# Raw attention scores of three chunks: two heads on the two row halves of the array, packed queries, narrower first tiles

## The chip, the cores and the metric

One core of a Trainium2 chip runs the whole program. The metric is the device time of one execution in microseconds (us), taken as the median of several runs. The engines are TensorE (PE, with its weight loads listed as PEld), VectorE (DVE), ScalarE (ACT), GpSimd (POOL) and SyncE (SP); SP and POOL also issue DMAs from their queues, in program order.

## What is computed

Sliding-window attention with a few sink columns, followed by a two-layer block over the 4 x 768 tokens. Cut to what matters:

```python
# q, k, v: (4, 8, 768, 64) float32; n_sink = 4, window = 128
scores = (q @ k.T) / 8                      # per head
keep = (pos_k < n_sink) | ((0 <= pos_q - pos_k) & (pos_q - pos_k < window))
a = exp(where(keep, scores, -1e9) - rowmax); a /= sum(a) + 1e-9
x = (a @ v) laid out as (3072, 512)         # 8 heads x 64 side by side
h = x @ w_in                                # (512, 2048)
out = (h - tanh(h)) @ w_out                 # (2048, 512)
```

## The kernel before, in words

**Work units.** The tokens are cut into 12 chunks of 256 (`NCHUNK`), each with 4 units (one per pair of heads), so unit `u` is chunk `u // 4`, head pair `u % 4`. The chunk list starts with the first chunks of three batches (chunks 0 to 2); those twelve units are the `raw(u)` ones (`RAW = 12`): their scores are one float32 matmul per head. All later units are first split into a rounded part and a rest (`split`, L464) and take two fp32r matmuls per head (L514).

**Scores of a unit** (`scores`, L497). A unit has two tiles of 128 queries, t = 0 and t = 1. The keys lie packed with the four sink columns repeated in front of every block (`TS = 132`, `WIN = 260`, `KW = 392` columns). A key tile holds the two heads of a pair in partitions 0 to 63 and 64 to 127. The query tile is `[128, 2, 256]`: for head h the other 64 partitions are zeros, so that a matmul over all 128 rows gives one head's scores:

```python
nc.tensor.matmul(ps[h][:, :WIN], lhsT=qt[u][:, h, t * P : (t + 1) * P],
                 rhs=kt[u][:, t * TS : t * TS + WIN], start=True, stop=True)
```

Head 0 goes to one PSUM bank and head 1 to another (banks s0 and s1 for t = 0, o0 and o1 for t = 1). `kind = min(2 * c + t, 2)`; for the raw units c = 0, so t = 0 is kind 0 and t = 1 is kind 1. `merge` on DVE (L529, L531) masks and takes the row minimum: with kind 0 it reads only columns 128 to 259 of the bank, with kind 1 it first copies columns 0 to 127 over others under a mask. Then ACT takes the exponent (L539), DVE the sums (L559, L560), ACT or POOL scales (L565, L569), POOL copies the sink columns (L574 to L576), PE transposes (L599), ACT, DVE and POOL mask and copy (L606, L613), and per two or four units `attend` (L632) does the sink and value matmuls: L656 over all 512 columns, L662 with 64 weight columns per head, so that the two heads of a pair lie on the two column halves of the array.

**Loads of a raw unit.** Units 0 and 1 are loaded ahead of the branch (L70 to L73) into `early`; `_load_pair` (L97) zeroes half of the query tile on POOL (L103) and sends one DMA per head (L104). For units 2 to 11, `load_qk` (L319) adds a POOL memset of the whole query tile (`zeros`, L348), a key DMA (L337) and `queries` (two DMAs, L344 by way of L104), both on SP. Units 4 to 11 lie in places lent by weight tiles that come later (`lent`, L309). For later units both loads go from POOL's queue (L337, L346).

**The two-layer block.** A step `n` is (chunk, weight group g of 8). Its first half is 24 fp32r matmuls of 256 columns (L793), then ACT and DVE form h - tanh(h) and split it (L812 to L821), and its second half is 12 matmuls of 512 columns (L863) or, from chunk `SA = 5` on, 21 matmuls of 256 columns (L897). The order starts with chunks 0, 1, 2 at g = 0, then at g = 1, then chunks 2 and 1 at each later g, then chunk 0 at g = 2 to 7, then chunks 3 to 11. The weights arrive as 64-bit words (L392) and are decoded on DVE in three passes (L156 to L160), rounded on ACT (L717) and their rest taken on DVE (L721). From chunk 3 on the first-layer weights are streamed from a scratch in DRAM by SP (L778) through seven ring blocks, four per step. From chunk 5 on the weights of the edge products are derived by SP and POOL DMAs, ACT and DVE (L982 to L1021). Results of the chunks 5 to 10 are stored from POOL's queue (`put`, L951, `ST = 1`).

**What sets the order.** `Work` (L169) is a planner at build time. Every piece of work has an engine, an estimated duration, a due time, and what it reads and writes. `order` (L194) plays the program: whenever an engine is free it takes, of the pieces that are ready, the one with the earliest due time; the resulting order is written out by hand on each engine. The due times come from the constants at L261 to L276 (`FIRST`, `EARLY`, `PACE`, `LEAD`, `LEAD3`, `UNIT`, `SECOND`, ...) by `due_step`, `due_unit` and `due_group`. So a constant does not delay work by itself; it decides which of several ready pieces goes first, and in what order a queue holds them.

Of the kernel before, what the change touches and what calls it, by code (L numbers as in the profile page):

```python
# [40 lines left out]
def kernel(  # L41
# [20 lines left out]
    for m in range(2):  # L62
        first = pts[:, m].rearrange("p h a b -> p (h a b)")
        early.append((first[:, :KW], first[:, KW : KW + 2 * CH].rearrange("p (h s) -> p h s", h=2)))
    et = mybir.EngineType
    with tc.manual_schedule(engines={et.PE, et.SP, et.DVE, et.Activation, et.Pool}):
# [3 lines left out]
        for m in range(2):  # L70
            k, q = early[m]
            nc.sync.dma_start(k, kp[0, m, :, :KW])
            _load_pair(nc, q, qd[0, 2 * m : 2 * m + 2, :, :CH], True)  # L73
            if m == 0:
                make_identity(nc, ident)
                nc.gpsimd.iota(scr[:, 0, :].bitcast(I32), pattern=[[-1, P]], base=0, channel_multiplier=1)
                nc.gpsimd.iota(scr[:, 1, :].bitcast(I32), pattern=[[1, P]], base=0, channel_multiplier=0)
# [19 lines left out]
def _load_pair(nc, q, src, zeros):  # L97


    for h in range(2):  # L100
        r, z = slice(64 * h, 64 * h + 64), slice(64 * (1 - h), 64 * (1 - h) + 64)
        if zeros:
            nc.gpsimd.memset(q[z, h, :], 0.0)  # L103
        nc.sync.dma_start(q[r, h, :], src[h, r])  # L104
# [128 lines left out]
def _banded(tc, qd, kp, vp, vs, masks, w_in, w_out, ident, pts, early, out):  # L233
    nc = tc.nc
    et = mybir.EngineType
    with ExitStack() as ctx:
# [25 lines left out]
        SLK, PAD, LATE, LAND, QP, KP, BP, LEAD3 = 0.0, 1.05, 65222.0, 4372.0, 0, 0, 1, 89032.0  # L262
        SA, NSLOT, RING, GP, LQ, ST = 5, 7, 7, 0, 1, 1
# [9 lines left out]
        FIRST, EARLY, PACE, LEAD = 45000.0, 4600.0, 8242.0, 72963.0  # L273
        UNIT, SECOND, WLEAD, WNEXT = 2000.0, 3000.0, 6000.0, 2500.0
        HALF2, LAST = 8269.0, 4401.0
        SPILL, STREAM, DEAR, DLATE = 54590.0, 4000.0, 39769.0, 31275.0  # L276
# [42 lines left out]
        def load_qk(u):  # L319
# [12 lines left out]
            def keys():  # L332
                if u in lent or u == 3:
                    kt[u] = lend()[:, 2 * CH : 2 * CH + KW]
                else:
                    kt[u] = kpool.tile([P, KW], F32, tag="kraw", name=f"kraw{u}")
                (nc.gpsimd if LQ and not raw(u) else nc.sync).dma_start(kt[u], kp[b, p, :, 2 * c * TS : 2 * c * TS + KW])  # L337

            def queries():
                if not raw(u):  # L340
                    qt[u] = qpool.tile([P, 2, CH], F32, tag="qraw", name=f"qraw{u}")
                src = qd[b, 2 * p : 2 * p + 2, :, c * CH : (c + 1) * CH]
                if raw(u):
                    _load_pair(nc, qt[u], src, False)  # L344
                else:
                    (nc.gpsimd if LQ else nc.sync).dma_start(qt[u], src.rearrange("h d s -> d h s"))  # L346

            def zeros():  # L348
                if u in lent or u == 3:
                    qt[u] = lend()[:, : 2 * CH].rearrange("p (h s) -> p h s", h=2)  # L350
                else:
                    qt[u] = qpool.tile([P, 2, CH], F32, tag="qraw", name=f"qraw{u}")
                nc.gpsimd.memset(qt[u], 0.0)

            t = due_unit(u) - 8000
            if raw(u):
                work.add("POOL", 460, t - ZL, zeros, (), [slots(u)[1]])
# [139 lines left out]
        def scores(u, t):  # L497
# [4 lines left out]
            def products():  # L502
                both = obank if apart else sbank if cc <= SA else txbank
                ps = sps[u, t] = both
                for h in range(2):
                    if raw(u):
                        nc.tensor.matmul(
                            ps[h][:, :WIN], lhsT=qt[u][:, h, t * P : (t + 1) * P],
                            rhs=kt[u][:, t * TS : t * TS + WIN], start=True, stop=True,
# [36 lines left out]
            if raw(u):  # L546
                src, took = slots(u), 890
# [433 lines left out]

        def derive(g, m):  # L982
# [24 lines left out]
            d = due_step(order.index((SA, g))) - DEAR if m != 6 else due_step(order.index((SA - 1, g))) + DLATE  # L1007
# [109 lines left out]
        for n in range(NS):  # L1117
# [6 lines left out]
            if n:  # L1124
# [6 lines left out]
                if cc == SA - 1:  # L1131
                    derive(g, 6)
# [216 lines left out]
```

## Time and profile before

| what | us |
|---|---|
| median of 3 runs (lowest, highest) | 685.65 (685.11, 689.05) |
| the profiled execution's own time | 685.92 |
| its span, first to last instruction | 684.2 |
| PE, DVE, ACT, POOL busy in it | 665.0, 531.4, 412.7, 204.7 |
| mean granted TensorE clock, share of full | 0.997 |

The profile is one execution. A busy share is an average over stages with different limits, and the ends of PE instructions are modelled, so a busy PE may still be waiting inside; the starts of successive PE rows are the safer reading. A float32 matmul shows as two records. In a timeline row the columns are start, length, engine, line, operation, output and inputs, shape, count, and in brackets the idle time before it with what ended it.

### The profile page before, as it was taken

Reading aid. Unit: us, or ns where it says so; the run is one execution under the profiler, and the core shown is the slowest. Engines: PE = TensorE matmul, PEld = TensorE weight load, DVE = VectorE, ACT = ScalarE, POOL = GpSimd, SP = SyncE. Lnnn points to the kernel's source line nnn. Section 1 sums busy time; section 2 is a strip of 40 time slices with the busy share of each in tenths; the row PEclk is TensorE's granted clock in tenths of the full one; section 3 lists DMA queues with packets and bytes.
Section 4 is the critical chain, followed back from the end, with each engine's and each line's share of the span. In section 5 each row is a group of like instructions: output and inputs, shape, how many; then the busy total and the mean of one; then the engine's idle time right before and its main releaser. Section 6 shows DMA issues by size and latency. Waiting matters only on the chain.

```text
span 684.2 us, 14570 instructions
## 1 busy us (share of the span) xinstructions
PE 665.0 (97%) x5099; PEld 613.8 (90%) x5099; DVE 531.4 (78%) x1365; ACT 412.7 (60%) x1056; POOL 204.7 (30%) x363
## 2 busy tenths in 40 slices
PE   6899999999999999999999999999999999999995
PEld 4677899989888898899999999999999999999995
DVE  6999988965998875577698797888888888755654
ACT  5986444435998876466676576676676567533331
POOL 5444000002985532334432323422223222300100
PEclk9999999999999999999999999999999999999998
DMA  6878896785999577799977767766667766656861
GB/s 178 269 252 273 283 308 242 285 280 155 199 209 289 182 228 222 216 290 284 265 223 215 230 176 233 231 209 207 215 216 231 245 192 168 206 160 196 261 187 35
DMA packets 79342, 152.96 MB, mean 224 GB/s; under 512 B 9565, under 2 KB 25565, under 8 KB 79261
## 3 DMA queue, kind: packets, MB, share of 16 engines
q1 hardware_dynamic: 65884, 121.65, 56.7%
q0 software_dynamic: 13376, 30.30, 16.4%
q8 instruction: 42, 0.69, 0.4%
q14 instruction: 40, 0.32, 0.1%
HBM read 131.47 MB, written 20.45 MB: 222 GB/s over the span
## 4 chain that ended last, share of the span: by engine, by line
PE 83%; POOL 4%; DVE 4%; ACT 4%; DMA 2%; issue 2%; SPq 0%; POOLq 0%; DVEq 0%; ACTq 0%
PE h L793 35%; PE s L897 11%; PE o L897 8%; PE o L863 8%; PE x L662 3%; PE s L863 3%; PE t L599 2%; PE t L662 2%; PE t L514 2%; PE t L863 2%; PE x L514 2%; PE x L863 2%; POOL edge L995 1%; PE s L514 1%; DMA v<-vp 1%
## 5 line engine op out<-in xcount | busy, mean ns | idle before, releaser
L793 PE MATMUL h<-xh,ring 128*128 128x256 f32 x660 | 133.5, 282 | 0.0
L812 ACT ACTIVATE gbuf<-h 128x512 f32<-128x512 f32 x96 | 57.2, 596 | 86.7 <-PE h L793 58.9
L793 PEld LDWEIGHTS h<-xh,ring 128*128 128x128 f32 x660 | 107.8, 188 | 0.4 <-PE t L662 0.2
L793 PE MATMUL h<-xh,spare 128*128 128x256 f32 x492 | 100.0, 283 | 0.0
L346 POOL DMA_DIRECT2D qraw<-qd x36 | 29.6, 821 | 222.7 <-DVE q L486 198.4
L793 PE MATMUL h<-xl,ring 128*128 128x256 f32 x330 | 92.2, 279 | 0.0
L539 ACT ACTIVATE p<-p,st 128x132 f32<-128x132 f32 x168 | 66.9, 400 | 27.8 <-DVE st L531 26.6
L831 ACT CAST ghbuf<-gbuf 128x896 fp32r<-128x896 f32 x55 | 51.8, 942 | 49.0 <-DVE gbuf L828 48.6
L793 PEld LDWEIGHTS h<-xh,spare 128*128 128x128 f32 x492 | 81.0, 190 | 0.3
L834 DVE TENSOR_TENSOR glbuf<-gbuf,ghbuf 128x896 fp32r<-128x896 f32 x55 | 60.3, 1097 | 20.1 <-ACT ghbuf L831 15.1
L793 PE MATMUL h<-xh,w 128*128 128x256 f32 x384 | 74.0, 282 | 0.0
L793 PE MATMUL h<-xl,spare 128*128 128x256 f32 x246 | 69.4, 282 | 0.0
L793 PEld LDWEIGHTS h<-xl,ring 128*128 128x128 f32 x330 | 62.1, 188 | 0.3
L793 PEld LDWEIGHTS h<-xh,w 128*128 128x128 f32 x384 | 61.1, 188 | 1.3 <-PE x L662 0.2
L565 ACT ACTIVATE p<-p,st 128x132 f32<-128x132 f32 x168 | 54.2, 394 | 3.5 <-DVE st L560 3.1
L815 DVE TENSOR_TENSOR gbuf<-h,gbuf 128x512 f32<-128x512 f32 x55 | 37.8, 687 | 21.9 <-ACT gbuf L812 21.3
L793 PE MATMUL h<-xl,w 128*128 128x256 f32 x192 | 53.8, 280 | 0.0
L619 POOL TENSOR_TENSOR pt<-pt,after 128x512 f32<-128x512 f32 x32 | 44.1, 1379 | 25.5 <-ACT pt L616 24.1
L863 PE MATMUL o<-w,ghbuf 128*128 128x512 f32 x192 | 50.8, 399 | 0.1
L793 PEld LDWEIGHTS h<-xl,spare 128*128 128x128 f32 x246 | 46.7, 190 | 0.3
L815 DVE TENSOR_TENSOR h<-h,gbuf 128x512 f32<-128x512 f32 x41 | 28.5, 695 | 19.1 <-ACT gbuf L812 19.0
L478 DVE TENSOR_TENSOR ks<-kraw,ks 64x392 fp32r<-64x392 f32 x72 | 40.5, 562 | 3.5 <-ACT ks L473 1.4
(174 smaller groups left out, 1693.2 us busy)
## 6 DMA issues: line engine op xcount, KB each, us to landing
ring<-wscr SPq DMA_DIRECT2D x165, 256.0 KB, 4.3
spare<-wscr SPq DMA_DIRECT2D x123, 256.0 KB, 4.5
qraw<-qd POOLq DMA_DIRECT2D x36, 256.0 KB, 5.2
wraw<-w_in SPq DMA_DIRECT2D x16, 512.0 KB, 6.4
wraw<-w_out SPq DMA_DIRECT2D x16, 512.0 KB, 6.9
wscr<-w SPq DMA_DIRECT2D x16, 512.0 KB, 6.0
kraw<-kp POOLq DMA_DIRECT2D x36, 196.0 KB, 4.5
v<-vp POOLq DMA_DIRECT2D x18, 256.0 KB, 3.3
```

Source lines behind the costliest of these rows:

```text
L478: (nc.gpsimd if KP else nc.vector).tensor_tensor(k[o, h, :], t[r, :], k[r, h, :].bitcast(F32), op=ALU.subtract)
L514: nc.tensor.matmul(ps[h][:, :WIN], lhsT=q[:, h, t * P : (t + 1) * P], rhs=rhs, start=i == 0, stop=i == 1,)
L539: nc.scalar.activation(e, e, AF.Exp, bias=st[u][:, j : j + 1], scale=-1.0, accum_out=st[u][:, 4 + j : 5 + j],)
L565: nc.scalar.activation(pr[u][:, j, :], pr[u][:, j, :], AF.Copy, scale=s[:, 8 + j : 9 + j])
L619: nc.gpsimd.tensor_tensor(w[:, :, 0, :], w[:, :, 0, :], after.unsqueeze(1).to_broadcast([P, 4, P]), op=ALU.mult)
L793: nc.tensor.matmul(hps[n][:, f, :], lhsT=w, rhs=x, start=r == 0, stop=r == 11)
L812: nc.scalar.activation(g0, h(), AF.Tanh)
L815: nc.vector.tensor_tensor(g0 if strassen(n) else h(), h(), g0, op=ALU.subtract)
L831: nc.scalar.copy(ghbuf[:, n % 2], gbuf[:, 1:, :])
L834: nc.vector.tensor_tensor(glbuf[:, :7, :], gbuf[:, 1:, :], ghbuf[:, n % 2].bitcast(F32), op=ALU.subtract)
L863: nc.tensor.matmul(sums_of(n, cc, t), lhsT=a[:, f, t * P : (t + 1) * P], rhs=wt[1, g][:, (0, 1, 0)[i], f, :], start=first and not low and ...
L897: nc.tensor.matmul(acc, lhsT=a[:, b, :], rhs=factor(g, m, part % 2), start=g == 0 and part == 0 and m in (4, 1, 2, 7), stop=closes(n) and ...
```

## The change

Units 0 to 11 keep their queries packed like the keys: 128 partitions, head 0 in the first 64 and head 1 in the last 64, with no zeros. One DMA brings both heads (the source holds each head's 64 rows twice, so that rows 64 to 191 of a pair are both heads in order). The POOL memsets go. A score matmul takes the 64 partitions of its head. For t = 0 it leaves out the first 128 columns, which `merge` does not read there, and the first 128 key columns are not loaded. The planner's durations for these products are 470 and 250 ns in place of 890, and 17 of its constants change: `LAND`, `LEAD3`, `FIRST`, `EARLY`, `PACE`, `LEAD`, `UNIT`, `SECOND`, `WLEAD`, `WNEXT`, `HALF2`, `LAST`, `SPILL`, `STREAM`, `DEAR`, `DLATE` and `ST` (with `ST = 0` the stores of chunks 5 to 10 and the reload `keep(True)` go from SP's queue instead of POOL's). `last_plain(g)` names the same step as the expression it replaces.

```diff
-        early.append((first[:, :KW], first[:, KW : KW + 2 * CH].rearrange("p (h s) -> p h s", h=2)))
+        early.append((first[:, :KW], first[:, KW : KW + CH]))
...
-            nc.sync.dma_start(k, kp[0, m, :, :KW])
-            _load_pair(nc, q, qd[0, 2 * m : 2 * m + 2, :, :CH], True)
+            nc.sync.dma_start(k[:, P:], kp[0, m, :, P:KW])
+            nc.sync.dma_start(q, _pair(qd, 0, m)[:, :CH])
...
-def _load_pair(nc, q, src, zeros):
...
+def _pair(qd, b, p):
+    return qd[b, 2 * p : 2 * p + 2].rearrange("h r s -> (h r) s")[D : 3 * D]
...
-        SLK, PAD, LATE, LAND, QP, KP, BP, LEAD3 = 0.0, 1.05, 65222.0, 4372.0, 0, 0, 1, 89032.0
-        SA, NSLOT, RING, GP, LQ, ST = 5, 7, 7, 0, 1, 1
+        SLK, PAD, LATE, LAND, QP, KP, BP, LEAD3 = 0.0, 1.05, 65222.0, 3413.0, 0, 0, 1, 126542.0
+        SA, NSLOT, RING, GP, LQ, ST = 5, 7, 7, 0, 1, 0
...
-        FIRST, EARLY, PACE, LEAD = 45000.0, 4600.0, 8242.0, 72963.0
-        UNIT, SECOND, WLEAD, WNEXT = 2000.0, 3000.0, 6000.0, 2500.0
-        HALF2, LAST = 8269.0, 4401.0
-        SPILL, STREAM, DEAR, DLATE = 54590.0, 4000.0, 39769.0, 31275.0
+        FIRST, EARLY, PACE, LEAD = 42195.0, 4733.0, 8116.0, 73377.0
+        UNIT, SECOND, WLEAD, WNEXT = 2018.0, 3598.0, 3159.0, 712.0
+        HALF2, LAST = 8566.0, 4470.0
+        SPILL, STREAM, DEAR, DLATE = 55847.0, 11745.0, 4846.0, 34199.0
...
+                a = P if raw(u) and not c else 0
+                (nc.gpsimd if LQ and not raw(u) else nc.sync).dma_start(
+                    kt[u][:, a:], kp[b, p, :, 2 * c * TS + a : 2 * c * TS + KW]
+                )
...
-            def zeros():
...
-                nc.gpsimd.memset(qt[u], 0.0)
+                nc.sync.dma_start(qt[u], _pair(qd, b, p)[:, c * CH : (c + 1) * CH])
...
-            if raw(u):
-                work.add("POOL", 460, t - ZL, zeros, (), [slots(u)[1]])
...
+                        r, a = slice(D * h, D * h + D), 0 if kind else P
                         nc.tensor.matmul(
-                            ps[h][:, :WIN], lhsT=qt[u][:, h, t * P : (t + 1) * P],
-                            rhs=kt[u][:, t * TS : t * TS + WIN], start=True, stop=True,
+                            ps[h][:, a:WIN], lhsT=qt[u][r, t * P : (t + 1) * P],
+                            rhs=kt[u][r, t * TS + a : t * TS + WIN], start=True, stop=True,
                         )
...
-                src, took = slots(u), 890
+                src, took = slots(u), 470 if kind else 250
...
+        def last_plain(g):
+            return max(n for n, (cc, x) in enumerate(order) if cc < SA and x == g)
...
-            d = due_step(order.index((SA, g))) - DEAR if m != 6 else due_step(order.index((SA - 1, g))) + DLATE
+            d = due_step(order.index((SA, g))) - DEAR if m != 6 else due_step(last_plain(g)) + DLATE
...
-                if cc == SA - 1:
+                if n - 1 == last_plain(g):
                     derive(g, 6)
```

## Rows read from the trace of the kernel before

**Rows 1.** The page, busy time by engine and granted clock in 40 slices.
```profile
PE 665.0 (97%) x5099; PEld 613.8 (90%) x5099; DVE 531.4 (78%) x1365; ACT 412.7 (60%) x1056; POOL 204.7 (30%) x363
...
PEclk9999999999999999999999999999999999999998
```
**Rows 2.** Busy time in four stretches: stretch, length, engines, clock, DMA share, GB/s.
```profile
8.00:56.00 48.00, 41.89 (x262) 31.80 (x263) 41.99 (x185) 43.41 (x166) 21.49 (x52) 1.00 0.81 258
56.00:80.00 24.00, 23.16 (x152) 19.20 (x153) 22.97 (x30) 10.56 (x20) 5.36 (x7) 1.00 0.86 295
80.00:145.00 65.00, 65.00 (x414) 58.59 (x413) 57.38 (x66) 27.45 (x41) 0.00 (x0) 1.00 0.80 274
145.00:676.00 531.00, 529.10 (x4259) 499.95 (x4258) 403.60 (x1067) 329.57 (x827) 172.11 (x283) 1.00 0.73 215
```
**Rows 3.** PE's timeline: score tile, transposes, value matmuls on column halves.
```profile
25.42 1.04 PE L507 MATMUL s<-qk 128*128 128x260 f32 x4
26.30 0.60 PE L599 MATMUL t<-ident,wide 128*128 128x128 f32 x4
26.74 0.38 PE L640 MATMUL x<-ident,z 128*128 128x128 f32 x2
...
38.27 1.52 PE L662 MATMUL x<-pt,v 128*64 128x256 f32 x16
39.72 0.49 PE L507 MATMUL s<-qk 128*128 128x260 f32 x1
```
**Rows 4.** The records of the score matmuls: ns min/median/max, first and last start.
```profile
L507 PE MATMUL s<-qk x36: 382/382/487, 14.2 to 48.4; 128*128 128x260 f32 x36
...
L507 PE MATMUL s<-pt x8: 382/564/802, 4.9 to 8.9; 128*128 128x260 f32 x8
```
**Rows 5.** Timeline of PE and ACT at the start and where a load is late.
```profile
4.95 2.10 PE L507 MATMUL s<-pt 128*128 128x260 f32 x4
6.84 1.25 PE L507 MATMUL o<-pt 128*128 128x260 f32 x4
...
8.11 0.41 ACT L539 ACTIVATE p<-p,st 128x132 f32<-128x132 f32 x1 [2.64 <-DVE st L531]
...
14.21 1.12 PE L507 MATMUL s<-qk 128*128 128x260 f32 x4 [1.29 <-DMA qk<-qd]
```
**Rows 6.** Timeline of POOL's memsets and SP's DMA issues from 5.9 us.
```profile
5.86 4.28 POOL L353 MEMSET qk<- 128x512 f32 x9
...
12.29 0.43 SPq L337 DMA_DIRECT2D qk<-kp  x1
12.81 1.14 SPq L104 DMA_DIRECT2D qk<-qd  x2
```
**Rows 7.** Busy time in four stretches of 4 us, columns as in rows 2.
```profile
12.00:16.00 4.00, 2.71 (x14) 2.01 (x13) 2.80 (x16) 2.27 (x12) 0.98 (x4) 1.00 0.79 251
16.00:20.00 4.00, 2.27 (x14) 1.87 (x14) 3.02 (x16) 4.00 (x16) 1.71 (x7) 1.00 0.78 229
...
24.00:28.00 4.00, 4.00 (x26) 3.00 (x22) 3.59 (x14) 3.39 (x12) 0.98 (x4) 1.00 1.00 309
...
40.00:44.00 4.00, 4.00 (x26) 3.60 (x26) 3.05 (x14) 2.33 (x9) 1.95 (x5) 1.00 0.98 289
```
**Rows 8.** ACT's waits from 20 to 65 us: total, times, longest.
```profile
ACT pt L606 <- PE t L599: 3.7, 3, 1.7
```
**Rows 9.** PE's timeline: chunk 2's values, and the last of steps 0 and 1.
```profile
61.67 1.52 PE L662 MATMUL x<-pt,v 128*64 128x256 f32 x16
...
63.93 2.03 PE L863 MATMUL s<-w,ghbuf 128*128 128x512 f32 x8
65.80 1.10 PE L863 MATMUL s<-w,glbuf 128*128 128x512 f32 x4
```
**Rows 10.** The decode's last pass on DVE, and PE's first matmul of step 16.
```profile
76.52 1.23 DVE L721 TENSOR_TENSOR w<-pt,w 128x1024 fp32r<-128x1024 f32 x1
...
143.39 1.22 DVE L721 TENSOR_TENSOR w<-pt,w 128x1024 fp32r<-128x1024 f32 x1
...
145.29 0.28 PE L793 MATMUL h<-xh,w 128*128 128x256 f32 x1
```
**Rows 11.** Waits of POOL's stores and of SP's ring loads: total, times, longest.
```profile
POOL out L954 <- DVE wide L949: 3.3, 5, 1.1
...
SPq L778 <- PE h L793: 236.5, 192, 6.9
```

More of the change, by code (lines that the diff above doesn't have):

```diff
@@ L94 @@
         _general(tc, qd, kp, vp, nswi, w_in, w_out, ident, xd, out)
-def _load_pair(nc, q, src, zeros):
[L100 to L104, printed above, removed]
+def _pair(qd, b, p):
+    return qd[b, 2 * p : 2 * p + 2].rearrange("h r s -> (h r) s")[D : 3 * D]
 def _masks(nc, pool, nswi, scr):
@@ L336, in keys @@
                     kt[u] = kpool.tile([P, KW], F32, tag="kraw", name=f"kraw{u}")
-                (nc.gpsimd if LQ and not raw(u) else nc.sync).dma_start(kt[u], kp[b, p, :, 2 * c * TS : 2 * c * TS + KW])
+                a = P if raw(u) and not c else 0
+                (nc.gpsimd if LQ and not raw(u) else nc.sync).dma_start(
+                    kt[u][:, a:], kp[b, p, :, 2 * c * TS + a : 2 * c * TS + KW]
+                )
             def queries():
@@ L341, in queries @@
                     qt[u] = qpool.tile([P, 2, CH], F32, tag="qraw", name=f"qraw{u}")
-                src = qd[b, 2 * p : 2 * p + 2, :, c * CH : (c + 1) * CH]
-                if raw(u):
-                    _load_pair(nc, qt[u], src, False)
-                else:
-                    (nc.gpsimd if LQ else nc.sync).dma_start(qt[u], src.rearrange("h d s -> d h s"))
-            def zeros():
[L349 to L352, printed above, removed]
-                nc.gpsimd.memset(qt[u], 0.0)
+                    src = qd[b, 2 * p : 2 * p + 2, :, c * CH : (c + 1) * CH]
+                    (nc.gpsimd if LQ else nc.sync).dma_start(qt[u], src.rearrange("h d s -> d h s"))
+                    return
+                if u in lent or u == 3:
+                    qt[u] = lend()[:, :CH]
+                else:
+                    qt[u] = qpool.tile([P, 2 * CH], F32, tag="qraw", name=f"qraw{u}")[:, :CH]
+                nc.sync.dma_start(qt[u], _pair(qd, b, p)[:, c * CH : (c + 1) * CH])
             t = due_unit(u) - 8000
-            if raw(u):
-                work.add("POOL", 460, t - ZL, zeros, (), [slots(u)[1]])
             e = "POOL" if LQ and not raw(u) else "SP"
```

## The prediction

> **What bounds the kernel now.** I read the page first, then busy time by stretch, then PE's timeline before 82 us, then the waits, then POOL's, SP's and DVE's timelines. The page says PE: 97% busy, at full granted clock in nearly every slice [rows 1]. By stretch it is finer [rows 2]. From 80 us on PE is full: 65.00 of 65, then 529.10 of 531. What it still has to do there is not touched by the change, so that part can only start earlier. From 8 to 56 us three engines share the bound: PE 41.89, DVE 41.99, ACT 43.41 of 48. That is where the 24 raw score tiles stand. So the question is not how much PE work goes, but how much earlier PE reaches the state it now has at 80 us.
>
> **PE's own saving.** A tile is four records; from 25.42 to the next operation at 26.30 it takes 0.88 us [rows 3], 24 tiles 21.1 us. The trace has no matmul on row halves. The nearest row is the value matmul, whose two heads lie on column halves: 16 records, half of them 256 and half 128 columns, in 39.72 - 38.27 = 1.45 us. One after another they would take 8 x 0.22 (0.88 / 4 for 260 columns) and 8 x 0.11 (four transposes of 128 columns, 26.30 to 26.74), 2.6 us [rows 3]. So halves do run side by side there, with 1.45 - 1.3 = 0.15 us over. By that row a tile of t = 1 (260 columns) falls from 0.88 to 0.44 and one of t = 0 (132 columns) to 0.22. Entering and leaving the mode costs something: the first record in front of which the weights could not be loaded ahead is 487 long against 382 [rows 4], 0.1 us, and this can come once on the way in and once on the way out, as 0 to 0.25 us a tile (more where tiles stand alone, nothing between neighbours). Freed: 12 x (0.44 + 0.66) = 13.2 us without switches, 24 x 0.25 = 6.0 less with all of them, 7.2. If row halves did not run side by side at all, t = 1 frees nothing and t = 0 frees 0.43: 5.2 less 6.0, about -1. I take 10, the middle of the two nearer ends.
>
> The column-half block shows what a change of mode costs: 0.15 us over its halves, and the tile behind it begins with a 0.49 us record [rows 3]. The Trainium skill has a rule that speaks against this change: switching the tiling mode, not just the tile, drains the engine (TensorEngine Tiling (Array Packing), Key Properties). It gives no time for it; the rows agree that something is lost at each border. If no score tile paid it, PE's saving would be 13.2, if all do 7.2.
>
> **What of it reaches the end.** Four terms, in order of time.
>
> 1. *Start, 1.2 us.* The first two tiles (t = 0, t = 1 of unit 0) take from 4.95 to 8.1, four records 1.89 us instead of 0.88: PE runs them at half speed, and ACT's first exponent waits 2.64 us to 8.11 [rows 5]. With 0.22 and 0.44 doubled they take about 1.3 us instead of 3; DVE can begin some 1.2 us earlier (bounds 0, if the loads land no sooner than now, and 2). Two query issues fewer and no zeroing ahead of the branch help the same point and are not counted twice.
>
> 2. *Loads, 0.4 us more.* From 8 to 16 us supply decides. PE waits 1.29 us for queries at 14.21 [rows 5], ACT has 2.27 busy of 4 [rows 7]. SP issues one key and two query DMAs per unit, 0.43 and 1.14 us [rows 6]; one query DMA instead of two saves 0.57, so unit 3 is some 1.1 earlier (units 2 and 3), unit 5 2.2. Keys shrink from 392 to 264 columns and the memsets of 4.28 us [rows 6] go; POOL has time there, so by themselves they are worth nothing. Against it: the first load of chunk 3's unit, two POOL DMAs of 128 partitions x (512 + 392) x 4 bytes, 0.46 MB, becomes due at once by `LEAD3` and may stand among these; at 251 GB/s [rows 7] that is 1.8 us of transfer. ACT is then fully busy from 16 us (4.00 of 4 [rows 7]). Lead at 20 us: 1.6 (bounds 0 and 3.5).
>
> 3. *The rest of the attention, 1.5 us.* From 20 to 56 us ACT does what it did before; it can only lose its idle time. Of the 4.59 us idle in 8 to 56 [rows 2], 1.73 lie in 12 to 16, counted above; 0.61 and 1.67 lie in 24 to 28 and 40 to 44 [rows 7], where it waits for transposes that stand behind score tiles on PE: 3.7 us in three waits [rows 8]. I take half of what is left, 1.5 (bounds 0 and 2.9). So chunk 2's values, now at 61.67 [rows 9], come 3.1 us earlier, while PE has about 10 us less to do until then.
>
> 4. *Filler, 2.8 us.* What PE does with the difference of 7 us: ahead of chunk 2's first half only steps 0 and 1 are there to be done, and of these the second half of step 1 (63.93 to 66.73 [rows 9]) still comes behind it today. It moves in front, 2.8 us; the remaining 4 us of freed PE time become idle. Bounds 0 (the planner leaves it behind) and 2.8.
>
> Sum: 1.2 + 0.4 + 1.5 + 2.8 = 5.9 us. From there PE runs as before, if the weights keep up. The decode of g = 2 ends at 77.75, some 9 us ahead of its use; the last ends at 144.6, 0.7 ahead of 145.29 [rows 10]. DVE gains the first 3.1 with the attention and has 7.6 us idle from 80 to 145 [rows 2] of which it needs 5.9 - 3.1 - 0.7 = 2.1, since in that stretch its gate work waits on PE, which is early. So I cost this at nothing; without it the gain stops at 3.8.
>
> The other edits: stores of six chunks and the last reload go to SP in front of ring loads. Twelve stores waited 3.3 us in five cases for DVE [rows 11], and SP's ring loads wait for PE to free blocks (236.5 us), not PE for them: hidden, else up to 2 us a chunk. `DEAR`, `DLATE` and the other due times reorder work from 145 us on, where PE has 1.9 us idle [rows 2]: they can gain at most that, and I take 0. The planner's order of the first 80 us also changes through all constants; I take that as the spread in terms 3 and 4.
>
> The profiled execution took 685.92 (span 684.2 and 1.7 around it): 685.92 - 5.9 = 680.0. The median stands 0.3 below it: **679.7 us**.
>
> **Rivals.**
>
> *PE's freed time counts in full.* The retuned order finds filler for nearly all of it, or spreads the attention so that ACT and DVE do not stop PE. For it: all three engines have 5 to 6 us idle in 8 to 56 [rows 2] and the decode has 9 us to give at g = 2 [rows 10]. Against it: ACT is full from 16 to 20 us [rows 7], and steps beyond 1 need chunk 2. Freed 10 to 13.2: 672.5 to 676.
>
> *Only the start moves.* ACT and DVE hold the attention where it is, filler stays behind chunk 2, or row halves do not run side by side: terms 1 and 2 alone, 1.6, or up to 2.5 with a little of the rest: 683 to 684.5. For it: DVE at 22.97 of 24 from 56 to 80 [rows 2], where the decode of g = 1 is due. That the halves don't overlap is in here, since the load and start terms stay.
>
> *The clock falls.* PE then stops more often before 56 us, and its granted clock drops from the 2.4 to the 1.2 level. For it: the first tiles already ran at half speed [rows 5]. Against it: 1.00 in 12 to 20 us with PE busy only 4.98 of 8 [rows 7], so stops of this size have not done it. PE has about 32 us of work left from 8 to 56; if half of it is slowed, 16 + 32 fill the 48 us and the gain is gone, 686; if all of it is, 64 us stand in place of 48, 702. It decides from that half on; I price it in the middle, 694. The Trainium skill says that an engine that idles is throttled again and must be warmed by activity (TensorE: Matmul & The Clock Gate, Part 1); by that rule gaps that grow would matter, and the trace has none so far that did it.
>
> *Stores in front of ring loads.* If at each of six chunk ends SP waits with the store until PE runs out of blocks, 1.5 to 2 us each, 9 to 12 in all against 5.9: 683 to 686, a little slower at worst. For it: ring loads are just in time (192 waits [rows 11]). Against it: the planner sees both queues, and no store waited over 1.1.
>
> **How the numbers follow.** A measurement of this kernel tells about 1% (6.9 us) from no change, so faster means below 678.8. Forecast, 676.5 to 683: 0.54, of which 0.23 below 678.8. Freed in full: 0.17, all faster. Only the start: 0.17, same. Clock: 0.06, 0.04 of it slower. Stores: 0.06, 0.02 slower. Faster 0.40, same 0.54, slower 0.06. Range 673.5 to 685.5: it leaves out the last part of the full case, the clock case and the worst of the stores.
>
> **What would show it.** Score tiles: two heads' records start within some ns of each other, a t = 1 tile stays under 0.7 us and a t = 0 tile under 0.5 up to the next operation. First exponent near 7 us. No wait for queries near 14 us. PE's busy share in 8 to 56 falls by several us while ACT's stays above 0.9. The second half of step 1 stands ahead of chunk 2's first half. PE idle from 80 us on stays at some 2 us, clock at 1.00. The forecast is wrong if the tiles keep 0.88, if the clock column falls below 0.95 before 56 us, if PE waits for the decode between 80 and 145, or if PE stays full before 56 us with all of its saving gone to the end.

## The result, and the profile after

The changed kernel takes 690.54 us (median of 20 runs) against 686.14 for the kernel before (20 runs): ratio 1.0059, 95% interval [1.0043, 1.0074]. It is slower by 0.6%, 4 us, where 5.9 us less had been forecast. The profiled execution has a span of 691.3 us, 7.2 more than before; it took 693.11 us, 2.6 above the median, so what is read from its trace below adds up to more than the 4 us of the medians.

The page of the changed kernel, busy time by engine and granted clock in 40 slices (as rows 1):
```profile
PE 667.4 (97%) x5099; PEld 610.1 (88%) x5099; DVE 534.3 (77%) x1365; ACT 415.1 (60%) x1056; POOL 188.8 (27%) x335
...
PEclk9979999999999999999999999999999999999999
```
PE has as many instructions as before and is busy 2.4 us longer, although 24 score tiles became shorter: the clock column has a hole in its third slice (35 to 52 us).

Busy time of the changed kernel in the four stretches of [rows 2] (columns as there):
```profile
8.00:56.00 48.00, 40.79 (x238) 27.41 (x239) 41.55 (x180) 41.09 (x155) 17.55 (x43) 0.89 0.69 217
56.00:80.00 24.00, 23.69 (x163) 19.87 (x163) 22.87 (x34) 13.64 (x32) 6.16 (x10) 1.00 0.80 284
80.00:145.00 65.00, 65.00 (x417) 58.71 (x416) 58.64 (x66) 28.28 (x41) 0.00 (x0) 1.00 0.80 274
145.00:676.00 531.00, 526.19 (x4217) 494.63 (x4216) 401.31 (x1060) 327.70 (x824) 163.23 (x269) 1.00 0.74 218
```
Four things differ from [rows 2]: in 8 to 56 us the clock is 0.89 and PE gets through 238 records instead of 262; ACT is down by 2.3 us, so it does its work later; from 56 to 80 there is more left to do on ACT; and from 145 us on PE idles 4.8 us where it had idled 1.9.

The reading that places the loss is the start of the hyperbolic tangents on ACT (L812 before, L806 after): each belongs to one step, the steps come in the same order in both kernels, and so the same step can be laid beside itself. "Lag" below is this difference to the kernel before, in us. The changed kernel's lag is +3.2 at step 0 (55 us), +2.1 at every step from 84 to 145 us, +0.9 at step 20 (171 us), +5.2 at step 36 (296 us), and then swings between 3 and 12 up to the last steps, where it is +7.2. So there are two losses: 2.1 us before 80 us, and 5.1 us from 175 us on, most of it by 350 us: in 300 to 350 us PE idles 2.2 us, where it had idled 0.04. A lag is the difference of two single executions. Of a kernel whose order up to 80 us is exactly that of the kernel before (the one with the landing time alone, below) the trace has +0.6 there, so lags below 1 us at 80 us tell little.

PE's timeline in the changed kernel, score tiles among the same neighbours as in [rows 3]:
```profile
23.52 0.50 PE L501 MATMUL s<-qk 64*128 64x132 f32 x4
23.85 0.60 PE L501 MATMUL o<-qk 64*128 64x260 f32 x4
...
29.49 0.71 PE L501 MATMUL o<-qk 64*128 64x260 f32 x4
30.03 0.39 PE L501 MATMUL s<-qk 64*128 64x132 f32 x4
30.98 1.25 PE L501 MATMUL o<-qk 64*128 64x260 f32 x4 [0.56 <-DVE st L525]
```
A t = 0 tile (132 columns) now takes 23.85 - 23.52 = 0.33 us up to the next operation and a t = 1 tile 30.03 - 29.49 = 0.54, against 0.88. The two heads' records start 6 or 7 ns apart. The products do what the change says: 12 x (0.55 + 0.34) = 10.7 us less PE work at this clock. The sum has limits: in front of first-layer products a t = 0 tile takes 0.43 us (from 50.26) and a t = 1 tile 0.64 (from 53.00), and the four records of the tile at 30.98 start 0.22 to 0.32 us apart, so that its heads do not run side by side at all.

The same view earlier, from the start:
```profile
4.87 0.81 PE L501 MATMUL s<-pt 64*128 64x132 f32 x4
5.47 1.08 PE L501 MATMUL o<-pt 64*128 64x260 f32 x4
...
12.66 1.41 PE L593 MATMUL t<-ident,p 128*128 128x128 f32 x4
13.99 0.81 PE L501 MATMUL s<-qk 64*128 64x132 f32 x4
14.60 1.08 PE L501 MATMUL o<-qk 64*128 64x260 f32 x4
...
17.09 1.12 PE L593 MATMUL t<-ident,p 128*128 128x128 f32 x4 [0.79 <-ACT pt L600]
```
Here the t = 0 tile takes 0.61 us and the group of four transposes 1.12 where [rows 3] has 0.60: every record is doubled. Before, records were doubled until 7 us; now until 22.5 us, and again from 33 to 39.7 and from 46.5 to 49.9. The tile at 13.99 no longer waits for queries (rows 5 had 1.29 us there).

The granted clock in stretches of 4 us (columns as in rows 7):
```profile
12.00:16.00 4.00, 3.98 (x17) 1.92 (x14) 3.23 (x20) 3.84 (x15) 1.63 (x7) 1.00 0.87 280
16.00:20.00 4.00, 3.02 (x14) 1.66 (x12) 3.15 (x16) 4.00 (x19) 1.52 (x6) 1.00 0.12 29
...
32.00:36.00 4.00, 2.33 (x14) 1.77 (x14) 3.59 (x18) 4.00 (x18) 0.92 (x4) 0.61 0.35 100
36.00:40.00 4.00, 3.96 (x21) 2.35 (x21) 3.52 (x15) 3.53 (x17) 1.93 (x4) 0.54 0.95 294
```
The clock column misses the first stretch of doubled records (it says 1.00 in 12 to 20 us) and shows the second. The trace has no record of the granted clock before 22.6 us (before 7.2 in the kernel before), and the column reads 1.00 where it has none. ACT is fuller from 12 to 16 us (3.84 against 2.27): the loads do come earlier. But in 16 to 20 us the DMA share is 0.12 where it was 0.78. SP's timeline in that place, and its waits from 3 to 70 us (total, times, longest), say why:
```profile
11.09 0.61 SPq L348 DMA_DIRECT2D qk<-qd  x1
17.98 0.61 SPq L429 DMA_DIRECT2D vraw<-vs  x1
...
22.27 7.44 SPq L374 DMA_DIRECT2D v<-vp  x2
```
```profile
SPq L374 <- PE x L656: 17.6, 3, 8.0
SPq L429 <- DVE vsink L444: 12.5, 3, 6.2
```
SP is through with its first unit loads at 11.7 us and then stands 6.2 us in front of the sink-row load, and later 7 us inside a pair of value loads, which wait for their buffers. These two waits were 11.9 and 5.0 us in all before.

PE's timeline at the end of the attention (as rows 9) and at step 16 (as rows 10):
```profile
64.87 1.52 PE L656 MATMUL x<-pt,v 128*64 128x256 f32 x16
...
67.13 2.03 PE L857 MATMUL s<-w,ghbuf 128*128 128x512 f32 x8
...
145.09 0.28 PE L787 MATMUL h<-xh,w 128*128 128x256 f32 x1
```
Chunk 2's values stand at 64.87, 3.2 us later than in [rows 9], and the second half of step 1 still comes behind them, at 67.13. The decode keeps up: PE has no idle time from 80 to 145.

Waits of the changed kernel from 145 to 400 us (PE's longest, then POOL's and ACT's on the derived weights):
```profile
PE t L508 <- DVE st L525: 1.5, 2, 0.9
...
PE s L508 <- DVE ks L471: 0.6, 1, 0.6
...
POOL edge L992 <- DMA edge<-bscr: 6.4, 1, 6.4
POOL w L992 <- PE x L508: 6.1, 2, 3.5
...
ACT w L995 <- DMA w<-bscr: 11.5, 6, 3.8
```
PE now waits for scores (L508): for `ks` and `st`, that is for a unit's keys and the masks behind it. And POOL, whose queue brings the keys and queries of the next units (L334, L342), stands in front of L992, the accumulating DMA of `derive`, which must follow SP's copy into the same block. Before, POOL's waits there in this stretch are 9.6 us on an edge block and 0.8 on another block, and ACT's 8.0. `LAND`, which the planner adds to a small time of each DMA (`lands`) to get its landing, went from 4372 to 3413 ns. For SP's copies ahead of L992 that makes 3.8 us (edge blocks) and 4.1 (the others) in place of 4.8 and 5.1; in the changed kernel these copies take a median of 4.5 and 4.8 us from issue to landing, in the kernel before 4.0 and 4.3.

### The profile page after: what moved, and what is told of

Same layout as the page of the kernel before. It is cut to its first block, busy times and chain, and to the rows that moved or that the text cites. A ratio compares the mean times of both kernels' runs of the same rounds, so it can differ in the third digit from the quotient of the medians.

```text
span 691.3 us, 14522 instructions
## 1 busy us (share of the span) xinstructions
PE 667.4 (97%) x5099; PEld 610.1 (88%) x5099; DVE 534.3 (77%) x1365; ACT 415.1 (60%) x1056; POOL 188.8 (27%) x335
## 4 chain that ended last, share of the span: by engine, by line
PE 76%; DVE 7%; DMA 5%; ACT 5%; issue 3%; POOL 1%; SPq 1%; DVEq 0%; POOLq 0%; ACTq 0%
PE h L787 33%; PE s L891 10%; PE o L891 7%; PE o L857 6%; PE s L857 3%; PE x L656 3%; PE t L593 2%; DMA kraw<-kp 2%; PE t L656 2%; PE t L508 2%; PE t L857 2%; PE x L857 2%; PE x L508 2%; DMA w<-bscr 1%; DVE pt L607 1%
## 5 line engine op out<-in xcount | busy, mean ns | idle before, releaser
L787 PE MATMUL h<-xh,ring 128*128 128x256 f32 x660 | 130.7, 281 | 0.4 <-DMA ring<-wscr 0.4
L806 ACT ACTIVATE gbuf<-h 128x512 f32<-128x512 f32 x96 | 57.1, 594 | 82.8 <-PE h L787 69.7
L342 POOL DMA_DIRECT2D qraw<-qd x36 | 28.9, 801 | 218.0 <-DVE q L479 165.9
L809 DVE TENSOR_TENSOR h<-h,gbuf 128x512 f32<-128x512 f32 x41 | 28.5, 696 | 22.8 <-ACT gbuf L806 22.6
```

Source lines behind the costliest of these rows:

```text
L787: nc.tensor.matmul(hps[n][:, f, :], lhsT=w, rhs=x, start=r == 0, stop=r == 11)
L806: nc.scalar.activation(g0, h(), AF.Tanh)
L809: nc.vector.tensor_tensor(g0 if strassen(n) else h(), h(), g0, op=ALU.subtract)
```

## The experiments

Three explanations stood against each other. *Order*: the planner, given other durations and constants, writes another order, and that order is worse. *Clock*: the shorter matmuls keep PE at the lower of its two levels. *Queue*: SP stands in front of waiting loads. For the early loss, a second question was why 10.7 us less PE work does not count.

**Old constants, new constants.** The changed kernel with the 17 old constants, and the kernel before with the 17 new ones:
```diff
-        SLK, PAD, LATE, LAND, QP, KP, BP, LEAD3 = 0.0, 1.05, 65222.0, 3413.0, 0, 0, 1, 126542.0
+        SLK, PAD, LATE, LAND, QP, KP, BP, LEAD3 = 0.0, 1.05, 65222.0, 4372.0, 0, 0, 1, 89032.0
...
```


> The changed kernel with all 17 planner constants of the kernel before; products, loads and the durations 470 and 250 stay as changed. Theory 'plan' (the new constants let PE wait between 145 and 420 us, some 4 to 5 us): about 686, and PE idle from 145 to 676 us falls from 4.8 to some 2 us. Theory 'clock' alone (all that was lost was lost to PE at the lower clock before 56 us): still about 690, and the idle after 145 us stays near 5.

Measured: 691.73 us, ratio 1.0070 [1.0054, 1.0085]. Lag +8.0 at 80 us and +6.9 at the end.

> The kernel before with the 17 new constants alone. Theory 'plan': 689 to 691, PE idle after 145 us 4 to 5 us, clock full before 56 us. Theory 'clock' alone: 686, as before.

Measured: 697.67 us, 1.0138 [1.0110, 1.0166]. Lag +0.8 at 80 us, +11.4 at the end; records doubled only to 6.8 us, as before.

Both from 145 us on (columns as in rows 2), old constants first:
```profile
145.00:676.00 531.00, 529.48 (x4257) 500.70 (x4256) 403.92 (x1064) 329.41 (x827) 171.91 (x283) 1.00 0.75 220
```
```profile
145.00:676.00 531.00, 523.32 (x4171) 493.22 (x4171) 399.55 (x1054) 325.70 (x822) 163.52 (x269) 0.99 0.73 215
```
This cuts the loss in two. With the old constants PE is as dense late as in [rows 2], and all is lost early. With the new ones nothing is lost early and PE idles 7.7 us late. So the late loss belongs to the constants and the early one to the products, the loads or the planned durations.

**Keeping PE busy.** Two full-row float32 matmuls on the identity, into unread columns, behind each raw tile; in the changed kernel and in the one with old constants:
```diff
+                        if h == 1:
+                            for _ in range(2):
+                                nc.tensor.matmul(ps[h][:, 384:], lhsT=ident, rhs=ident, start=True, stop=True)
```


> The changed kernel with two more float32 matmuls of 128 columns over all 128 rows behind each raw score tile, into columns of the bank that nothing reads (24 x 0.44 us at the full clock); the planner's durations are left, so the order is that of the changed kernel. Theory 'clock' (the array is too little used in 8 to 56 us and the clock stays low or falls): the double distances between records after 8 us go, the granted clock reads 1.00 in all stretches, and PE reaches 80 us 2 to 4 us earlier: 686 to 688. If the clock is not what costs: 24 x 0.44 = 10.6 us more on PE, of which some reaches the end: 692 to 700.

Measured: 694.02, 1.0110 [1.0089, 1.0131]; lag +5.3 at 80 us.

> The changed kernel with the constants of before and the same added matmuls. If both theories hold the two gains add: 682 to 684, under the kernel before. If only the plan counts: 686 or above. If only the clock: about 687.

Measured: 693.17, 1.0096 [1.0069, 1.0122]; lag +10.6 at 80 us.

In the first, records are doubled until 18.5 us (in the second until 24) and not again before the end, and both are slower all the same: the fill work costs more than the clock gives back. Since these matmuls add work, the two runs do not by themselves clear the clock.

**A longer warm-up.** `WARM` 10 in place of 3 (dummy matmuls ahead of the first loads), on three kernels:
```diff
-        WARM = 3
+        WARM = 10
```


> The changed kernel with 10 warm-up matmuls ahead of the branch in place of 3, nothing else. The double distances of the records end at 7.3 us in the kernel before, at some 22 us in the changed one. Theory 'clock at the start' (too little of the array is used between 3 and 22 us): records at full distance from some 7 to 8 us on, SP no longer waits in 12 to 18 us, chunk work earlier by 3 us or more at 55 us; the loss after 145 us stays, so 687 to 688. If row-half matmuls bring the clock down again soon: double distances come back within 10 us and the time stays near 690. If the clock is no cause: 690 to 692, later by what the warm-up takes.

Measured: 690.56, 1.0061 [1.0041, 1.0082]; lag +1.7 at 80 us (2.1 without). SP's two waits stay (17.5 and 14.0 us).

> The same with all constants of before, where nothing was lost after 80 us. By 'clock at the start': the 8 us of lag at 80 us of the first run with these constants go to 2 or less, 684 to 686. If SP's waits in the middle (12 to 18, 22 to 30 us) come from the order and not from a slow PE: still some 8 us late, 691.

Measured: 692.18, 1.0090 [1.0064, 1.0117]; lag +6.8 (8.0 without).

> As the run before with one full-row float32 matmul of 128 columns (0.22 us) behind every raw tile, to hold the clock where PE has gaps. If the clock falls again at 33 to 43 us without it: this one is 2 to 4 us faster than the run before, 681 to 683. If the clock holds anyway: 0 to 3 us slower than it.

Measured: 692.43, 1.0086 [1.0063, 1.0109]; lag +7.1.

Full clock comes at 9.4 us instead of 22.5 in the first and third, and at 7 in the second, but it does not last. In the first, records are doubled again from 20.8 to 25.6 and 36 to 42.6, in the third from 36.8 to 39.7 and 78 to 81.5, in the second from 14 to 24, 34 to 37.5, 58 to 61.4 and 78.5 to 82. So the longer warm-up takes away 8 to 10 us at the lower clock in the first two, and what this brings back up to 80 us is 0.4 and 1.2 us. The clock at the start is a small cost; later falls are not cured here.

**Narrow first tiles alone.** The kernel before, its t = 0 products without the first 128 columns, planned at 890 and 450 ns:
```diff
-                            ps[h][:, :WIN], lhsT=qt[u][:, h, t * P : (t + 1) * P],
-                            rhs=kt[u][:, t * TS : t * TS + WIN], start=True, stop=True,
+                            ps[h][:, a:WIN], lhsT=qt[u][:, h, t * P : (t + 1) * P],
+                            rhs=kt[u][:, t * TS + a : t * TS + WIN], start=True, stop=True,
...
-                src, took = slots(u), 890
+                src, took = slots(u), 890 if kind else 450
```


> The kernel before, queries with zeros and all rows, its constants; only the t = 0 products leave out the first 128 columns (12 x 0.43 us less on PE), planned at 450 ns. If what brings the clock down is PE's shorter work as such: double distances last longer than 7.3 us or come back, 686 to 690. If it is the half-used rows: clock full from 7.3 us on as before, 683 to 686.

Measured: 686.17, 1.000 [0.999, 1.001]; lag +0.8 at 80 us; granted clock 0.66 in 16 to 20 us. Twelve tiles, planned 440 ns shorter each, free some 5 us of PE and move nothing; the shorter plan also wrote a slightly different order. The lower clock in 16 to 20 us is no sign of the narrower products: it was granted from 17.3 to 20.7 us here, but also from 19.1 to 22.5 and from 18.2 to 21.6 in two of the kernels below whose products are those of before (the landing time alone; ACT's scaling left out).

**The changed products in the order of before.** The changed products, queries and loads, but the planner is told what it was told before (old constants, 890 ns, an empty POOL piece of 460 ns), so that every engine's order is that of before:
```diff
-                src, took = slots(u), 470 if kind else 250
+                src, took = slots(u), 890
```


> The changed products and loads, but the planner is told what it was told before (all constants of before, 890 ns a product, an empty 460 ns piece on POOL where the zeroing was), so that every engine's order is exactly that of the kernel before. Theory 'order' (the work is re-ordered by the shorter durations so that SP and PE wait at other points; the products by themselves gain something): PE reaches 80 us 1 to 4 us earlier than before, 682 to 685. Theory 'clock' (row-half products leave PE at the lower clock up to 22 us and that costs by itself): 5 to 8 us late at 80 us as with the old constants, 691 to 693. If PE's time does not count in that stretch at all: 686, like before.

Measured: 685.93, 0.9993 [0.9973, 1.0014]. Chunk 2's values at 60.68 us; lag -1.0 from step 0 to 180 us. In the traces every engine's work stands in the order of the kernel before, POOL's without the zeroing.

> The same with 10 warm-up matmuls. If the lower clock up to 22 us costs even in the order of before: 1 to 3 us under the run before this. If not: the same within 1 us.

Measured (the same with `WARM` 10): 687.50, 1.0006 [0.9986, 1.0026]; lag +1.0 at 80 us, 2.0 later than without the longer warm-up. Here too the full clock, from 8 us on, is lost again from 18 to 25 and from 35 to 42 us.

The first of these is the run that decides: the same products, doubled records until 22.4 us and from 36.9 to 39.6, a DMA share of 0.34 in 16 to 20 us, SP's two waits at 15.5 and 8.9 us (24 together; 30 in the changed kernel, 17 before), and no loss. So the products, their loads and the lower clock at the start do not by themselves make a kernel slower than the one before; it takes the new order. Nor do the products make it faster, by more than 1.0 us at 80. What this run does not have is 6.8 us more at the lower clock between 33 and 50 us and another 6 us of SP's waits. No run takes either out of the changed kernel alone, so how much of its 2.1 us the order costs through them stays open.

The profiled execution of this run is the slowest of the twelve (689.21) and loses 3.0 us between 296 and 350 us with the order unchanged:
```profile
300.00:310.00 10.00, 8.43 (x55) 7.41 (x54) 5.56 (x18) 4.67 (x12) 3.07 (x5) 0.97 0.99 271
310.00:320.00 10.00, 10.00 (x53) 8.67 (x52) 5.86 (x11) 6.68 (x17) 5.58 (x8) 0.86 0.83 224
```
PE idles 1.6 us, 1.5 of it in one wait for a mask of DVE (until 308.2), and then the clock is at its lower level from 309.4 to 312.9 us. Why this wait comes up in some executions stays open.

**The new durations alone, the new landing time alone**, each as the only edit to the kernel before:
```diff
-                src, took = slots(u), 890
+                src, took = slots(u), 470 if kind else 250
```


> The kernel before, its products and loads untouched, only the planner's durations of the raw products at 470 and 250 ns in place of 890. Theory 'order': the order alone loses, 689 to 693, with SP waiting longer than before in 10 to 60 us. If the loss comes from the clock or the products: 686 to 687.

Measured: 692.33, 1.0078 [1.0053, 1.0104]. Lag -2.6 at step 0, +4.2 at step 2, +6.3 from step 4 to the end.

```diff
-        SLK, PAD, LATE, LAND, QP, KP, BP, LEAD3 = 0.0, 1.05, 65222.0, 4372.0, 0, 0, 1, 89032.0
+        SLK, PAD, LATE, LAND, QP, KP, BP, LEAD3 = 0.0, 1.05, 65222.0, 3413.0, 0, 0, 1, 89032.0
```


> The kernel before with one constant changed: LAND 3413 in place of 4372, the planner's time for a DMA to land after 65 us. If this is what lets POOL wait for landings ahead of the next unit's loads (3.5 to 4.4 us each near 300 us in the changed kernel): 4 to 10 us lost after 145 us, 690 to 697. If the loss with all new constants (697.7) lies with another one (ST, LEAD3, DEAR): 685 to 687.

Measured: 691.91, 1.0074 [1.0053, 1.0095]. Lag +0.6 at 80 us, -0.4 at 171, +7.8 at 314, +6.4 at the end.

Neither edit changes any work, only an order, and each costs 6 us by itself. With the durations alone, the stretch from 56 to 80 us, and PE's timeline at chunk 2's values:
```profile
56.00:80.00 24.00, 20.66 (x122) 16.45 (x123) 20.99 (x29) 11.69 (x24) 7.16 (x9) 0.87 0.80 280
```
```profile
64.87 1.09 PE L863 MATMUL s<-w,ghbuf 128*128 128x512 f32 x4
...
66.12 1.52 PE L662 MATMUL x<-pt,v 128*64 128x256 f32 x16
67.57 1.20 PE L863 MATMUL s<-w,ghbuf 128*128 128x512 f32 x4
```
The planner believes PE to be free early and puts steps 0 and 1 in front; chunk 2's values slide from 61.67 to 66.12, and behind them PE has nothing left to fill its waits with: 3.3 us idle where [rows 2] has 0.8. The 0.87 in the row is part of the price. Two stretches of 4 us of the same run:
```profile
56.00:60.00 4.00, 3.41 (x17) 2.13 (x19) 3.56 (x6) 3.09 (x9) 3.62 (x6) 0.61 0.85 264
...
76.00:80.00 4.00, 2.59 (x6) 2.13 (x7) 4.00 (x6) 2.27 (x4) 0.00 (x0) 0.68 0.99 398
```
Twice PE stands for more than 2 us (2.1 until 56.6, behind a copy on ACT; 2.7 until 77.4, behind a rounding on ACT), and right after each wait the granted clock is at its lower level for 3.4 us, from 56.9 and from 77.4 us. PE works through both stretches at half speed, so by estimate 3.4 us of its work are lost to the clock beside the idle time. The kernel before has no such fall there. In this way the clock is one of the means by which an order costs, though not the reason.

With the landing time alone, the stretch from 145 us and POOL's waits from 145 to 400 us:
```profile
145.00:676.00 531.00, 526.02 (x4214) 495.87 (x4214) 401.09 (x1058) 328.13 (x824) 171.83 (x283) 1.00 0.74 215
```
```profile
POOL w L995 <- PE h L793: 8.7, 2, 4.6
POOL w L995 <- DMA w<-bscr: 7.0, 4, 3.6
...
POOL w L995 <- PE x L514: 4.5, 1, 4.5
```
The same kind of waits of POOL in front of the accumulating DMA as in the changed kernel, and nearly the same PE idle time, 5.0 us. Here PE idles 2.1 us between 181 and 186 us, and from 186.4 to 189.8 the clock is at its lower level. In sum POOL waits 36.7 us in front of this DMA from 145 to 400 us here, 36.5 in the changed kernel, 35.7 with all new constants and the old products, but 10.4 in the kernel before, 11.8 with the old constants and the new products. That these waits are the link is read from the traces; no run takes them out alone.

**Less ACT work, with PE's work old and new.** ACT's scaling of nine of the first twelve units left out (10.8 us as planned), in the kernel before and in the one with the order of before:
```diff
-                work.add("ACT", 1200, d + 500, scale, [("st", u % 4)], ps)
+                work.add("ACT", 1200, d + 500, (lambda: None) if raw(u) else scale, [("st", u % 4)], ps)
```


> The kernel before without ACT's scaling of the first 12 units' probabilities by the reciprocal row sums (nine units, 36 instructions, 10.8 us of ACT; the pieces stay in the plan, so the order is that of before; the output lacks that scaling). Theory 'ACT bounds 8 to 56 us': chunk 2's values, now at 61.7, come 4 to 8 us earlier, 678 to 682. If PE or the loads bound that stretch with the old products: 0 to 2 us earlier, 684 to 686.

Measured: 685.49, 0.9986 [0.9967, 1.0005]; lag +0.2 at 80 us.

> The same left out of the kernel with the changed products in the order of before. If ACT hid PE's saving: this one is 2 to 5 us faster than the run before this, 674 to 679. If the saving is lost for another reason (lower clock, SP's waits): no more than 1 us faster than the run before this.

Measured: 683.63, 0.9956 [0.9939, 0.9973]; lag -3.2 at 80 us; chunk 2's values at 58.40.

8 to 56 us in both, the kernel before without scaling first:
```profile
8.00:56.00 48.00, 42.82 (x261) 32.99 (x260) 41.33 (x185) 34.42 (x130) 19.87 (x52) 0.96 0.79 253
```
```profile
8.00:56.00 48.00, 43.12 (x283) 30.65 (x284) 44.45 (x190) 36.25 (x134) 20.61 (x50) 0.96 0.79 258
```
Nine us less on ACT alone move the attention by nothing (+0.2). The changed products and loads alone move it by 1.0 us; the two together by 3.2. With both, DVE rises to 44.45 of 48. PE's longest wait from 8 to 56 us in the kernel before without scaling:
```profile
PE s L507 <- DMA qk<-qd: 3.6, 2, 2.6
```
There PE waits 3.6 us for queries, where it had waited 1.3 [rows 5]; with the new loads and without scaling it waits 0.6. So this stretch has no single bound whose relief counts: with ACT relieved the loads hold it in part, and whether the 3.2 us come from PE's shorter work or from the single query DMA is not shown, since every run with the packed queries has both.

**The landing time put back in the changed kernel:**
```diff
-        SLK, PAD, LATE, LAND, QP, KP, BP, LEAD3 = 0.0, 1.05, 65222.0, 3413.0, 0, 0, 1, 126542.0
+        SLK, PAD, LATE, LAND, QP, KP, BP, LEAD3 = 0.0, 1.05, 65222.0, 4372.0, 0, 0, 1, 126542.0
```


> The changed kernel with LAND at 4372 again, the other 16 constants new. If LAND makes most of the loss after 145 us (5 us in the changed kernel): 685 to 687, PE idle from 145 to 676 us near 2. If the others (ST, LEAD3, DEAR) make it: 689 to 691.

Measured: 687.75, 1.0006 [0.9984, 1.0029]; lag +1.8 at 80 us, +2.6 at the end.
```profile
145.00:676.00 531.00, 526.65 (x4255) 499.18 (x4254) 402.04 (x1062) 330.73 (x827) 163.25 (x269) 1.00 0.74 218
```
By the lag, 0.8 us are lost late where it was 5.1; the median falls by 2.8 us. PE passes 4255 records in the stretch where the changed kernel passed 4217, though its idle time is nearly as long (4.4 against 4.8). The difference lies inside the records: from 145 us to the end of the span PE is busy 530.31 us before, 534.65 in the changed kernel and 530.47 here, for 4263, 4273 and 4271 records. So some 4 us in which PE counts as busy in the changed kernel can only be waits inside the records; 3.6 of them lie in the scores (L508) and transposes (L593) of later units, 73.63 us there and 70.00 here for the same 432 records. The other new constants and the stores on SP are still in, so in this execution those cost 0.8 us late.

**A version with ACT relieved without leaving work out.** The order of before, with every fourth early unit's scaling moved to POOL:
```diff
-        RAW, TWO, CUT, DUO, SC, PB, ZL, TK = 12, 12, 2, 3, 4, 4, -4000, 1100
+        RAW, TWO, CUT, DUO, SC, PB, ZL, TK = 12, 12, 2, 3, 3, 4, -4000, 1100
```


> The changed products with the planner told what it was told before, and SC at 3 in place of 4: four of the twelve units scaled on POOL in place of three, 1.2 us less on ACT, 1.1 more on POOL. If ACT is the limit and the order does not get worse: 1 us earlier at chunk 2's values, 684 to 685.5. If the re-planning costs as in the other runs: 688 to 693.

Measured: 684.74, 0.9975 [0.9957, 0.9992]; lag -1.4 at 80 us, -2.4 at 171. It beats both kernels, by 1.5 and by 6 us, of which the first is hardly more than can be told apart. Its profiled execution (688.52, the slowest of ten) has the same loss near 300 us as the run with the order of before: PE idles 1.6 us from 300 to 310, and the clock is lower from 308.7 to 312.1.

## Why the prediction was wrong, point by point

- **PE's own saving** (10, between 7.2 and 13.2): right, 10.7 at full clock for tiles among score tiles and transposes. The 0.33 and 0.54 us are each 0.10 to 0.11 above the halved columns (0.22, 0.44); in front of first-layer products it is 0.2 (0.43 and 0.64), within the 0 to 0.25 a tile of the prediction. The Trainium skill has the rule that a change of the tiling mode drains the engine (TensorEngine Tiling (Array Packing), Key Properties). These tiles agree with it, and no run separates the drain from the weight loads. That a tile's heads can also stand one behind the other (30.98) was not in the sum.
- **Start** (1.2): failed. The first exponent stays at 8.11 in the changed kernel. Both first tiles run doubled, as the term had it, and by the trace PE is through with them at 6.5 us; but DVE's first mask operation begins at 7.77, as before. The term took DVE to wait for PE. In both traces DVE itself is at its own loads of the branch's condition (L79, to 7.07 us) and at the branch (L91, to 7.6). In the order of before DVE comes to them 0.4 us earlier and the first exponent at 7.69, at most a third of the term.
- **Loads** (0.4 more): the wait for queries at 14 us went, and ACT was full 4 us sooner, but the lead was given back. SP reaches the sink-row and value loads earlier and stands longer in front of them, since their buffers become free at PE's and DVE's pace. The term counted what SP issues and not what it next waits for.
- **The rest of the attention** (1.5, chunk 2's values 3.1 us earlier): failed in its sign. They came 3.2 us later in the changed kernel and 1.0 us earlier in the order of before. The step behind it, that PE's saving removes ACT's 3.7 us of waits [rows 8], took ACT for the bound; without the scaling, 9 us less of ACT moved nothing either, and PE then waited longer for queries (3.6 us instead of 1.3).
- **Filler** (2.8): failed. The second half of step 1 stands behind chunk 2's values as before, and the new order moves steps 0 and 1 later (lag +3.2), not earlier.
- **"The planner's order of the first 80 us also changes through all constants; I take that as the spread in terms 3 and 4"**: this is the step that failed for the early part. An order is no spread about a mean. New durations with all old constants cost 6.3 us with the old products and 8.0 with the new; in the changed kernel 2.1 are left. That the other new constants take 6 us of it back follows from old and new constants laid side by side, and no run separated which of them do.
- **"`DEAR`, `DLATE` and the other due times ... can gain at most that, and I take 0"**: this failed for the late part. PE's 1.9 us of idle time bounds what an order can gain there and nothing bounds what it can lose. `LAND` stands in the list of changed constants and had no term: alone it cost 6.4 us, and putting it back returned 4.3 of the 5.1 in the profiled executions, 2.8 us in the medians.
- **Decode, at nothing**: right, PE is full from 80 to 145. **Stores** as a rival: not seen; with all other new constants they cost 0.8 us late once `LAND` was put back.
- **The clock** as a rival: half right. It fell, to 0.89 over 8 to 56 us, one of the named signs, and the price put on it was far too high there: 0.4 to 1.2 us for 8 to 10 us less of it in the warm-up runs, where 14 us (694 against 680) had been named, since the stretch mostly hides it. What it costs where it falls behind a wait after 56 us, as with the durations alone, had no term.
- **Only the start moves** came nearest for the products by themselves (1.0 us with the order of before), but by other terms.

## What to carry to other kernels

Where a build-time planner writes the order, a duration or a landing time in it is an edit to the whole kernel: run the new work once in the old order and the new order once with the old work, and price them apart. An idle share bounds what a reordering can win and says nothing of what it can lose. Here copies planned at 3.8 and 4.1 us that took medians of 3.6 to 4.8 left GpSimd's queue standing some 36 us in front of a DMA with the next loads behind it; planned at 4.8 and 5.1 it stood 10 to 19 us. Only these two values were run. Where three engines are each 87 to 90% busy in a stretch, take one engine's work away in an experiment before counting its saving: here 10.7 us of PE with the lighter loads gave 1.0, 9 us of ACT gave nothing, and both gave 3.2.

## What the runs showed of the hardware that was not expected

With score matmuls on 64 rows PE stayed longer at its lower level (1.2 of 2.4 GHz) at the start, although it hardly stopped. Without fill matmuls or a longer warm-up, six traces with 128-row products have records at full distance from 7 to 9 us on, and six with 64-row products from 15 to 23. With the fill matmuls PE is busy 4.00 of 4 us in three stretches running (columns as in rows 2):
```profile
8.00:12.00 4.00, 4.00 (x18) 2.82 (x16) 1.80 (x10) 2.51 (x12) 0.00 (x0) 1.00 0.97 290
12.00:16.00 4.00, 4.00 (x18) 2.87 (x16) 2.45 (x16) 2.27 (x8) 0.00 (x0) 1.00 0.83 270
16.00:20.00 4.00, 4.00 (x25) 2.87 (x22) 2.50 (x13) 3.95 (x18) 2.54 (x9) 1.00 0.05 17
```
and its timeline still has doubled records until 18 us:
```profile
16.38 1.22 PE L507 MATMUL o<-ident 128*128 128x128 f32 x4
17.39 0.78 PE L596 MATMUL t<-ident,p 128*128 128x128 f32 x4
18.11 0.50 PE L501 MATMUL s<-qk 64*128 64x132 f32 x4
18.53 0.71 PE L507 MATMUL s<-ident 128*128 128x128 f32 x4
```
The four identity records that take 1.01 us from 16.38 to the next operation take 0.64 from 18.53 on. The Trainium skill ties the lower level to an idle engine (TensorE: Matmul & The Clock Gate, Part 1); by busy time this trace does not agree. It is a finding of traces side by side; no run changes the rows of the products and nothing else. And the clock column reads 1.00 in all these early stretches, because the trace has no record of the clock yet, so at the start of a kernel the distance between records is the safer witness.

Later falls came behind waits of PE: 2.1 and 2.7 us with the durations alone (lower from 56.9 and 77.4 us), 1.5 us in the order of before (lower from 309.4). Each time records were doubled for 3.4 us, though PE was at work again. Not every wait brings one: in the kernel before PE stands 1.7 us until 17.9 and the clock stays up.
